# Next operands made later and over more steps, low part last, products in source order

## The chip, the cores and the metric

One core of a Trainium2 chip runs the whole program in one launch. The metric is the device time of one execution in microseconds (us). The kernel before was timed three times: 1541.97 us in the middle, 1541.9 and 1543.53 at the ends.

## The reference, cut to what matters

Attention with pooled keys and values gives tokens x (4608 x 512). Then come two stages of matrix products without biases:

```python
a = x @ w1; b = x @ w2
x2 = (a * b @ w3) @ w_out          # moe_*: d_ff 1024
h = x2 @ w_in                      # moe2_*: 512 x 2048
r = np.maximum(h, 0.0)
out = (r * r) @ w_out2             # moe2_w_out: 2048 x 512
```

All is float32. The change touches the last three lines alone.

## The kernel before

Tokens are cut into nine blocks of 512. A float32 operand is split into a high part, which is the value rounded to the type that TensorE takes (made by ScalarE, a cast), and a low part, the remainder (made by VectorE, a subtraction); `split` (L118 to L120) does both. A product of two operands is three matrix products: high x high, high x low, low x high.

The second stage takes the blocks in pairs (p = 0 to 3; the ninth block is left without a partner and goes last). For a pair, the products with w_in and with w_out are each done by seven products of combinations instead of eight. For w_in, `h_step(p, u, n)` does product n = 0 to 6 of unit u = 0 to 7: six products of 128x128 by 128x512 into one accumulator (ps_a to ps_d), then sums, relu and square, which leave a tile gs. Its moving operands `x2o` are seven combinations B11, T1, T2, T3, B21, B22, T4 of the pair's x2, for two halves each. `operands_of(p)` returns a list: one load, then one `cut` per name. A cut is, for two halves, a difference in place (only for T1 to T4; L1043) and a `split`. So the seven cuts are 8 differences and 14 low parts on VectorE and 14 casts on ScalarE. The tiles x2o have no second set: T1 of the next pair is written over T1 of this one, after its last product.

For w_out, `o_step(p, m, u)` does product m = 0 to 6 of unit u = 0 to 7: three products into each of two accumulators o (L1174). Its moving operand `gt` (high and low part of a gs or of a difference of two gs, which is L1148) is made by `o_prep`, three steps ahead; `cuts` is the list of the low parts made so far. After unit 7 of an m the accumulators are added to sums `so` (L1189, or copied at first by ScalarE, L1205), and for m = 3 to 6 a sum is transposed (L1195) and stored.

Stationary operands come from DRAM through a ring of eight tiles `un`: a step's unit is fetched eight steps ahead, when the step that had the tile has ended. SP issues these loads and all other loads and stores of this part.

`plan()` sets the order of steps: for pair p, the last of the steps with w_in, then one or two steps with w_out that are left over, then twelve steps with w_out of the pair (m = 0 for u = 0 to 7, then m = 1 for u = 0 to 3), then w_in of the next pair in turn with w_out of this one. I call this place a change of pairs. The first (from pair 0 to pair 1) has no w_out left over; in the second and third, one step (m = 6, u = 7) stands ahead of the twelve, so that the ninth of the twelve, (m = 1, u = 0), is the tenth from there.

A scheduler of the framework then orders each engine's instructions: it takes the source's order, but lets an instruction that it thinks ready go ahead of one that it thinks is not. `issue_after(ins, other)` ties one instruction behind another of the same engine, without a wait. The main loop calls the cuts: before, at n = 1, 3, 4, 5, 6 of the last unit and at two later steps with w_out.

Of the kernel before, what the change touches and what calls it, by code (L numbers as in the profile page):

```python
# [15 lines left out]
P = 128  # L16
# [19 lines left out]
def attn_moe_moe2_kernel(  # L36
# [16 lines left out]
    nc = tc.nc  # L53
# [47 lines left out]
    def tick():  # L101
        ticks[0] += 1
        for p in list(pumps):
            p()
# [9 lines left out]
    def f32(ap):  # L114
        return ap.bitcast(F32)

    def split(hi, lo, src, eng=None):

        nc.scalar.copy(hi, src)  # L119
        return (eng or nc.vector).tensor_sub(lo, src, f32(hi))  # L120

    def issue_after(ins, other):

        tc.add_manual_dep(
            ins.ins, other.ins.name, mybir.DependencyInfo(
                mybir.DependencyClass.NoSync, mybir.DependencyReason.DATA),
            reason="queue order")
# [46 lines left out]
    def run_step(steps):  # L174
        for fn in steps.pop(0):
            fn()
# [42 lines left out]
    def fetch():  # L219
        if n_used[0] + len(ahead) < len(useq):  # L220
            key = useq[n_used[0] + len(ahead)]
            while key not in stored:
                run_step(quarters)
            r = ring[0].tile([P, 2, 2, P], F32R, tag="unit", name="un")
            nc.sync.dma_start(f32(r), unit(key))
            ahead.append(r)

    def fetched(key):
        assert useq[n_used[0]] == key, (useq[n_used[0]], key)
        n_used[0] += 1  # L230
        return ahead.pop(0)
# [608 lines left out]
    NU = F2 // P // 2  # L840
# [79 lines left out]
    def out_unit(key):  # L920
        return key.rearrange("p a b c -> p (a b c)").rearrange("p (i c) -> p i c", i=2)
# [41 lines left out]
    def plain_units(u):  # L963
        half, v = divmod(u, NU)
        return [(("A11", "A12"), ("A21", "A22"))[half][x] for x in range(2)], v
# [47 lines left out]
    def drop(name):  # L1013
        slots.append(gs.pop(name))
# [5 lines left out]
    def operands_of(p):  # L1020

        iA, iB = pairs[p]
        raws = {}

        def load():
            for i in range(2):
                for y in range(2):
                    r = raw_x[0] if i and y else raw_p.tile(
                        [P, 2, TB], F32, tag="raw", name="x2r")
                    for x, blk in enumerate((iA, iB)):  # L1030
                        nc.sync.dma_start(r[:, x, :], x2d[blk][:, 2 * y + i, :])
                    raws[i, y] = r

        def cut(name):

            y, x = {"B21": (1, 0), "B22": (1, 1), "T3": (0, 1)}.get(name, (0, 0))
            for i in range(2):
                src = raws[i, y][:, x]
                a, b = {"T1": (raws[i, 0][:, 1], src), "T2": (raws[i, 1][:, 1], src),
                        "T3": (raws[i, 1][:, 1], src), "T4": (raws[i, 1][:, 0], src)}.get(  # L1040
                            name, (None, None))
                if a is not None:
                    nc.vector.tensor_sub(src, a, b)  # L1043
                t = x2o[name, i]
                split(t[:, 0, :], t[:, 1, :], src)

        return [load] + [
            (lambda n=n: cut(n)) for n in ("B11", "T1", "T2", "T3", "B21", "B22", "T4")]

    def plain_operands():  # L1050
        raws = []

        def load():
            for y in range(2):
                r = raw_p.tile([P, 2, TB], F32, tag="raw", name="x2r")
                nc.sync.dma_start(r, x2d[last][:, 2 * y:2 * y + 2, :])
                raws.append(r)

        def cut(kc):
            t = x2o[PLAIN[kc]]  # L1060
            split(t[:, 0, :], t[:, 1, :], raws[kc // 2][:, kc % 2])

        return [load] + [(lambda kc=kc: cut(kc)) for kc in range(KD)]
# [2 lines left out]


    hb = {}

    def run_prods(ps, todo, first):  # L1070
        for j, (l, r) in enumerate(todo):
            nc.tensor.matmul(ps, l, r, start=first and j == 0, stop=j == len(todo) - 1,  # L1072
                             skip_group_check=True)
        fetch()
        tick()

# [58 lines left out]
    ob = {}  # L1135
# [19 lines left out]
    cuts = []  # L1155
# [3 lines left out]
    def sub(t, x):  # L1159


        return t.rearrange("p (j x a) -> p j x a", x=2, a=32)[:, :, x, :]

    def o_step(p, m, u):
        name, x = OPRODS[m]
        if u == 0 and m < 2:
            ob[x] = [ps_acc.tile([P, TB], F32, tag="acc", name=f"o{x}") for _ in range(2)]
        un = out_unit(fetched(("o" + name, u)))
        gt = gts.pop(("o", p, m, u))
        for o in range(2):  # L1170
            os_ = slice(o * P, (o + 1) * P)
            todo = [(un[:, 0, os_], gt[:, 0]), (un[:, 0, os_], gt[:, 1]), (un[:, 1, os_], gt[:, 0])]
            for j, (l, r) in enumerate(todo):
                nc.tensor.matmul(  # L1174
                    ob[x][o], l, r, start=u == 0 and m != 5 and j == 0,
                    stop=u == NU - 1 and j == 2, skip_group_check=True)
        fetch()
        tick()
        g = {2: 2, 4: 1, 5: 4, 6: 3}.get(m)
        if g:  # L1180
            drop((p, u, g))
        if u < NU - 1:
            return
        iA, iB = pairs[p]

        def add(to, src):
            for o in range(2):
                ps = ob[x][o].rearrange("p (j a) -> p j a", a=32)
                nc.vector.tensor_add(sub(sums_o[to], o), ps, sub(sums_o[src], o))  # L1189

        def finish(name, blk, half):

            add(name, name)
            r = sums_o[4]
            nc.vector.transpose(r, sums_o[name])  # L1195
            for i in range(P // 32):
                c0 = i * P + half * 64
                nc.sync.dma_start(
                    out[blk * TB:(blk + 1) * TB, c0:c0 + 64].rearrange("(j a) c -> a j c", a=32),
                    r[i * 32:(i + 1) * 32].rearrange("p (j c) -> p j c", c=64))  # L1200


        if m == 0:
            for o in range(2):
                nc.scalar.copy(sub(sums_o[0], o), ob[x][o].rearrange("p (j a) -> p j a", a=32))  # L1205
        elif m == 1:
            add(1, 0)
        elif m == 2:
            add(2, 0)
            add(3, 1)  # L1210
        elif m == 3:
            add(2, 2)
            finish(3, iB, 1)
        elif m == 4:
            finish(2, iA, 1)
        elif m == 5:
            finish(1, iB, 0)
        else:
            finish(0, iA, 0)
# [99 lines left out]
    for step in order:  # L1319
# [4 lines left out]
        elif step[0] == "ph":  # L1324
            names, x = plain_units(step[2])
# [57 lines left out]
    def prepare():  # L1383
        while n_prep[0] < min(n_out + 3, len(outs)) and ready(outs[n_prep[0]]):
            o_prep(outs[n_prep[0]])
            n_prep[0] += 1

    todo_x = []
    head = False
    for step in order:  # L1390
        if step[0] == "h":
            _, p, u, n = step
            h_step(p, u, n)
            prepare()
            nxt = p + 1
            if u == NU - 2 and n == 0:
                todo_x = operands_of(nxt) if nxt < len(pairs) else plain_operands()
                todo_x.pop(0)()
            if u == 0 and n == 0:
                assert not todo_x  # L1400
                head = False
            if u == NU - 1 and n in (1, 3, 4, 5, 6) and todo_x:
                todo_x.pop(0)()
                head = n == 6
        elif step[0] == "ph":
            ph_step(*step[1:])
            prepare()
        else:
            if step[:3] == ("o", 0, 0) and step[3] == 0:
                while quarters:  # L1410
                    run_step(quarters)
                for _ in range(4):
                    t = prep_p.tile([P, 2, TB], F32, tag="w", name="so")
                    sums_o.insert(0, t.rearrange("p x c -> p (x c)"))
            prepare()
            n_out += 1
            if todo_x and head and step[2:] in ((0, 2), (0, 5), (1, 1), (1, 3)):
                todo_x.pop(0)()
            (o_step if step[0] == "o" else po_step)(*step[1:])
    for p in reversed(late):  # L1420
# [33 lines left out]
```

## Time and profile before

| what | value |
|---|---|
| median of three runs | 1541.97 us |
| the profiled execution | 1548.74 us |
| its span, first to last instruction | 1546.9 us |
| TensorE (PE) busy | 1496.1 us, 97% |
| VectorE (DVE) busy | 986.8 us, 64% |
| ScalarE (ACT) busy | 780.7 us, 50% |
| products and weight loads | 6752 each |

The profile was taken from one execution. A matrix product's record lasts 0.39 us since products overlap; the time that one takes is the distance from start to start. A bracket behind a row of a timeline is idle time ahead of it and what ended it. A count in a window holds every instruction that touches it.

### The profile page before, as it was taken

How to read it: one execution, taken by the hardware profiler on the slowest of the kernel's cores; microseconds unless marked ns; L12 is line 12 of the kernel's file. 1: busy time of each engine (PE TensorE's matmuls, PEld its weight loads, DVE VectorE, ACT ScalarE, POOL GpSimd, SP SyncE). 2: the span in 40 equal slices, each digit the busy share in tenths (PEclk: the TensorE clock that was granted, in tenths of full speed). 3: DMA queues.
4: the chain of work that ended last, by engine and by line, in shares of the span. 5: the costliest groups of instructions: out<-in, count | busy, mean ns of one | idle time of the engine just before them, and what ended most of it. 6: DMA issues, size and time to landing. Idle time of an engine off the chain costs nothing.

```text
span 1546.9 us, 21467 instructions
## 1 busy us (share of the span) xinstructions
PE 1496.1 (97%) x6752; PEld 1199.4 (78%) x6752; DVE 986.8 (64%) x1778; ACT 780.7 (50%) x1905; POOL 82.5 (5%) x146
## 2 busy tenths in 40 slices
PE   5899999989999999999999999999999999999998
PEld 3457777868887888778888777888888888888887
DVE  7897685646666565667245467758775877476642
ACT  6766454434453453646134664456445644464441
POOL 1011011101010010100000000000000000000000
PEclk9999999999999999999999999999999999999999
DMA  9555656646574855777429768778777877798752
GB/s 296 185 156 140 168 175 165 180 121 182 153 223 117 269 159 159 212 227 244 134 90 304 215 185 242 196 218 224 239 203 213 228 209 208 206 269 281 209 161 93
DMA packets 304720, 303.85 MB, mean 196 GB/s; under 512 B 131296, under 2 KB 196832, under 8 KB 304608
## 3 DMA queue, kind: packets, MB, share of 16 engines
q1 hardware_dynamic: 299424, 293.04, 65.3%
q10 hardware_dynamic: 5184, 9.44, 1.7%
q8 instruction: 55, 0.90, 0.3%
q14 instruction: 57, 0.47, 0.1%
HBM read 243.27 MB, written 56.62 MB: 194 GB/s over the span
## 4 chain that ended last, share of the span: by engine, by line
PE 67%; DMA 4%; DVE 4%; ACT 2%; SPq 1%; issue 1%; DVEq 0%; ACTq 0%
PE o L1174 17%; PE ps_w L185 16%; PE acc L185 8%; PE ps_a L1072 5%; PE ps_c L1072 5%; PE ps_d L1072 5%; PE ps_h L185 3%; PE o L185 3%; PE ps_b L1072 2%; DMA raw<-in_moe_w_out_dram 1%; PE ps_s L439 1%; PE ps_av L185 1%; DVE x2o L120 1%; PE ps_t L486 1%; DMA x2d<-st 1%
## 5 line engine op out<-in xcount | busy, mean ns | idle before, releaser
L1174 PE MATMUL o<-gt,un 128*128 128x512 f32 x1344 | 329.7, 390 | 1.4 <-DVE gt L120 1.0
L1174 PEld LDWEIGHTS o<-gt,un 128*128 128x128 f32 x1344 | 251.8, 188 | 55.8 <-DVE gt L120 3.5
L120 DVE TENSOR_TENSOR gt<-gs,gt 128x512 fp32r<-128x512 f32 x240 | 164.7, 688 | 184.0 <-ACT gt L119 182.4
L185 PE MATMUL ps_w<-x,wt 128*128 128x512 f32 x960 | 243.3, 399 | 2.7 <-ACT x L517 1.9
L119 ACT CAST gt<-gs 128x512 fp32r<-128x512 f32 x240 | 148.6, 620 | 156.3 <-PE o L1174 89.8
L185 PE MATMUL acc<-gt,Wt 128*128 128x512 f32 x864 | 219.4, 396 | 3.0 <-ACT st L829 2.8
L185 PEld LDWEIGHTS ps_w<-x,wt 128*128 128x128 f32 x960 | 176.5, 189 | 42.1 <-DVE x L520 3.3
L185 PE MATMUL ps_w<-x,un 128*128 128x512 f32 x768 | 187.9, 393 | 0.0
L185 PEld LDWEIGHTS acc<-gt,Wt 128*128 128x128 f32 x864 | 160.0, 189 | 35.8 <-ACT st L829 4.0
L185 PEld LDWEIGHTS ps_w<-x,un 128*128 128x128 f32 x768 | 142.0, 188 | 29.6 <-issue 1.2
L456 ACT ACTIVATE att<-ps_s,mx 128x72 f32<-128x72 f32 (+1 forms) x320 | 98.0, 324 | 65.0 <-DVE mx L454 64.3
L1079 ACT ACTIVATE r<-r 128x512 f32<-128x512 f32 x96 | 60.6, 632 | 120.0 <-DVE r L1109 119.4
L801 DVE TENSOR_TENSOR gf<-asb,ps_w 128x512 f32<-128x512 f32 x72 | 49.3, 684 | 88.0 <-PE ps_w L185 87.5
L1072 PE MATMUL ps_a<-x2o,un 128*128 128x512 f32 x384 | 98.3, 391 | 3.7 <-ACT p L1097 2.2
L1072 PE MATMUL ps_c<-x2o,un 128*128 128x512 f32 x384 | 98.7, 393 | 0.0
L1072 PE MATMUL ps_d<-x2o,un 128*128 128x512 f32 x384 | 97.7, 390 | 0.0
L119 ACT CAST gt<-gf 128x512 fp32r<-128x512 f32 x72 | 44.8, 623 | 94.0 <-DVE gf L801 92.8
L1080 ACT ACTIVATE gs<-r 128x512 f32<-128x512 f32 x144 | 89.9, 629 | 1.7
L1072 PEld LDWEIGHTS ps_a<-x2o,un 128*128 128x128 f32 x384 | 71.9, 188 | 19.7 <-ACT p L1097 2.6
L1148 DVE TENSOR_TENSOR gs<-gs 128x512 f32<-128x512 f32 x128 | 86.6, 683 | 0.0
L1072 PEld LDWEIGHTS ps_c<-x2o,un 128*128 128x128 f32 x384 | 72.8, 190 | 15.4 <-DVE u L1103 0.3
L1072 PEld LDWEIGHTS ps_d<-x2o,un 128*128 128x128 f32 x384 | 72.4, 189 | 15.1
(109 smaller groups left out, 1943.3 us busy)
## 6 DMA issues: line engine op xcount, KB each, us to landing
un<-u_w SPq DMA_DIRECT2D x128, 256.0 KB
un<-u_A SPq DMA_DIRECT2D x128, 256.0 KB
un<-u_S SPq DMA_DIRECT2D x128, 256.0 KB
un<-u_oS SPq DMA_DIRECT2D x128, 256.0 KB
un<-u_oA SPq DMA_DIRECT2D x96, 256.0 KB
raw<-in_moe_w_dram SPq DMA_DIRECT2D x32, 512.0 KB
raw<-in_moe_w_out_dram SPq DMA_DIRECT2D x24, 512.0 KB
x2d<-st ACTq DMA_DIRECT2D x36, 256.0 KB
```

What stands on the lines that cost most here:

```text
L119: nc.scalar.copy(hi, src)
L120: return (eng or nc.vector).tensor_sub(lo, src, f32(hi))
L185: (lambda a=a, b=b, i=i: nc.tensor.matmul(ps, a, b, start=first and i == 0, stop=last and i == n - 1))
L439: nc.tensor.matmul(ps[:n, x * 2 * SP:(x + 1) * 2 * SP], t[:, hp, c0:c0 + n], kbd[:, hp].rearrange("p a s -> p (a s)"), start=True, stop=True)
L456: nc.scalar.activation(av[:, h0 + h], sv[:, h], ACTF.Exp, bias=mx[:n, h:h + 1], scale=scale, accum_out=sm[:n, h0 + h:h0 + h + 1])
L486: nc.tensor.transpose(ps[:, c, :n], att[g % 2][:n, c * 2 * SP:c * 2 * SP + P], ident[:n, :n])
L801: nc.vector.tensor_mul(gf, asb, pss[1])
L1072: nc.tensor.matmul(ps, l, r, start=first and j == 0, stop=j == len(todo) - 1, skip_group_check=True)
L1079: nc.scalar.activation(t, src, ACTF.Relu)
L1080: nc.scalar.activation(take(name), t, ACTF.Square)
L1148: d = nc.vector.tensor_sub(src, a, src)
L1174: nc.tensor.matmul(ob[x][o], l, r, start=u == 0 and m != 5 and j == 0, stop=u == NU - 1 and j == 2, skip_group_check=True)
```

## The change

Four edits. The main loop makes the next pair's operands at n = 1, 3, 5 of the last unit (B11, T1, T2) and at the steps with w_out m = 0, u = 0, 2, 3, 5 (T3, B21, B22, T4). The first instruction of a cut on VectorE is tied behind the newest low part of a gt. In a step with w_out the products go high x high, low of the weights x high, high x low of gt, each for both accumulators in turn, so that gt's low part is read last. All products of `h_step` and `o_step` are tied into the source's order.

```diff
--- before.py
+++ after.py
@@ -1039,10 +1039,13 @@
                 a, b = {"T1": (raws[i, 0][:, 1], src), "T2": (raws[i, 1][:, 1], src),
                         "T3": (raws[i, 1][:, 1], src), "T4": (raws[i, 1][:, 0], src)}.get(
                             name, (None, None))
+                d = []
                 if a is not None:
-                    nc.vector.tensor_sub(src, a, b)
+                    d.append(nc.vector.tensor_sub(src, a, b))
                 t = x2o[name, i]
-                split(t[:, 0, :], t[:, 1, :], src)
+                d.append(split(t[:, 0, :], t[:, 1, :], src))
+                if cuts:
+                    issue_after(d[0], cuts[-1])
 
         return [load] + [
             (lambda n=n: cut(n)) for n in ("B11", "T1", "T2", "T3", "B21", "B22", "T4")]
@@ -1066,11 +1069,19 @@
 
 
     hb = {}
+    last_mm = []
+
+    def in_turn(ins):
+
+        if last_mm:
+            issue_after(ins, last_mm[0])
+        last_mm[:] = [ins]
 
     def run_prods(ps, todo, first):
         for j, (l, r) in enumerate(todo):
-            nc.tensor.matmul(ps, l, r, start=first and j == 0, stop=j == len(todo) - 1,
-                             skip_group_check=True)
+            in_turn(nc.tensor.matmul(
+                ps, l, r, start=first and j == 0, stop=j == len(todo) - 1,
+                skip_group_check=True))
         fetch()
         tick()
 
@@ -1167,13 +1178,12 @@
             ob[x] = [ps_acc.tile([P, TB], F32, tag="acc", name=f"o{x}") for _ in range(2)]
         un = out_unit(fetched(("o" + name, u)))
         gt = gts.pop(("o", p, m, u))
-        for o in range(2):
-            os_ = slice(o * P, (o + 1) * P)
-            todo = [(un[:, 0, os_], gt[:, 0]), (un[:, 0, os_], gt[:, 1]), (un[:, 1, os_], gt[:, 0])]
-            for j, (l, r) in enumerate(todo):
-                nc.tensor.matmul(
-                    ob[x][o], l, r, start=u == 0 and m != 5 and j == 0,
-                    stop=u == NU - 1 and j == 2, skip_group_check=True)
+        for j, (x1, x2) in enumerate(((0, 0), (1, 0), (0, 1))):
+            for o in range(2):
+                in_turn(nc.tensor.matmul(
+                    ob[x][o], un[:, x1, o * P:(o + 1) * P], gt[:, x2],
+                    start=u == 0 and m != 5 and j == 0,
+                    stop=u == NU - 1 and j == 2, skip_group_check=True))
         fetch()
         tick()
         g = {2: 2, 4: 1, 5: 4, 6: 3}.get(m)
@@ -1399,9 +1409,10 @@
             if u == 0 and n == 0:
                 assert not todo_x
                 head = False
-            if u == NU - 1 and n in (1, 3, 4, 5, 6) and todo_x:
+            if u == NU - 1 and n in (1, 3, 5) and todo_x:
                 todo_x.pop(0)()
-                head = n == 6
+            if u == NU - 1 and n == 6:
+                head = True
         elif step[0] == "ph":
             ph_step(*step[1:])
             prepare()
@@ -1414,7 +1425,7 @@
                     sums_o.insert(0, t.rearrange("p x c -> p (x c)"))
             prepare()
             n_out += 1
-            if todo_x and head and step[2:] in ((0, 2), (0, 5), (1, 1), (1, 3)):
+            if todo_x and head and step[2:] in ((0, 0), (0, 2), (0, 3), (0, 5)):
                 todo_x.pop(0)()
             (o_step if step[0] == "o" else po_step)(*step[1:])
     for p in reversed(late):
```

On TensorE, at the first change of pairs, the order before puts products of the new pair (ps_a) behind the eighth step with w_out (gt_9134 is its operand, gt_9152 that of the ninth):

```order
L1174 MATMUL o_9077<-gt_9134,un 128x512 x3
L1072 MATMUL ps_a<-x2o,un 128x512 x3
L1174 MATMUL o_9181<-gt_9152,un 128x512
L1174 MATMUL o_9182<-gt_9152,un 128x512
L1072 MATMUL ps_a<-x2o,un 128x512 x2
L1174 MATMUL o_9181<-gt_9152,un 128x512 x2
L1174 MATMUL o_9182<-gt_9152,un 128x512 x2
L1174 MATMUL o_9181<-gt_9164,un 128x512 x3
```

After, they stand behind the twelfth step, whose operand is gt_9192 (gt_9178 is the eleventh's):

```order
L1183 MATMUL o_9182<-gt_9178,un 128x512
L1183 MATMUL o_9181<-gt_9192,un 128x512
L1183 MATMUL o_9182<-gt_9192,un 128x512
L1183 MATMUL o_9181<-gt_9192,un 128x512
L1183 MATMUL o_9182<-gt_9192,un 128x512
L1183 MATMUL o_9181<-gt_9192,un 128x512
L1183 MATMUL o_9182<-gt_9192,un 128x512
L1082 MATMUL ps_a<-x2o,un 128x512 x6
L1082 MATMUL ps_b<-x2o,un 128x512 x6
```

Nowhere else does the order of steps on TensorE change; within a step with w_out the two accumulators take turns.

On VectorE, at the second change of pairs, this stands before from the low part of the fourth step with w_out (gt_10471) to that of the ninth (gt_10537); x2o rows are low parts of operands, x2r rows their differences, the gs row is a difference of two gs:

```order
L120 TENSOR_TENSOR gt_10471<-gs,gt_10471 128x512
L120 TENSOR_TENSOR gt_10482<-gs,gt_10482 128x512
L120 TENSOR_TENSOR x2o<-x2r,x2o 128x512
L120 TENSOR_TENSOR gt_10497<-gs,gt_10497 128x512
L120 TENSOR_TENSOR x2o<-x2r,x2o 128x512
L1043 TENSOR_TENSOR x2r<-x2r 128x512
L120 TENSOR_TENSOR gt_10508<-gs,gt_10508 128x512
L1148 TENSOR_TENSOR gs<-gs 128x512
L120 TENSOR_TENSOR x2o<-x2r,x2o 128x512
L120 TENSOR_TENSOR gt_10519<-gs,gt_10519 128x512
L120 TENSOR_TENSOR gt_10537<-gs,gt_10537 128x512
```

After, from the fourth step (gt_10467) to the ninth (gt_10537):

```order
L120 TENSOR_TENSOR gt_10467<-gs,gt_10467 128x512
L120 TENSOR_TENSOR x2o<-x2r,x2o 128x512 x2
L120 TENSOR_TENSOR gt_10478<-gs,gt_10478 128x512
L120 TENSOR_TENSOR x2o<-x2r,x2o 128x512 x2
L120 TENSOR_TENSOR gt_10493<-gs,gt_10493 128x512
L120 TENSOR_TENSOR x2o<-x2r,x2o 128x512 x2
L120 TENSOR_TENSOR gt_10508<-gs,gt_10508 128x512
L120 TENSOR_TENSOR gt_10519<-gs,gt_10519 128x512
L1044 TENSOR_TENSOR x2r<-x2r 128x512 x2
L1159 TENSOR_TENSOR gs<-gs 128x512
L120 TENSOR_TENSOR x2o<-x2r,x2o 128x512 x2
L120 TENSOR_TENSOR gt_10537<-gs,gt_10537 128x512
```

Eleven instructions were between and at these ends, and now seventeen; two more, a pair of x2r, now stand between the transpose (L1205 after, L1195 before) and the first of these rows. Between them and the two sums ahead of the transpose nothing else moved. The third change has the same order.

## Rows read from the trace of the kernel before

**Rows 1.** page: busy time; costliest line (busy, mean ns, idle before)

```profile
PE 1496.1 (97%) x6752; PEld 1199.4 (78%) x6752; DVE 986.8 (64%) x1778; ACT 780.7 (50%) x1905; POOL 82.5 (5%) x146
...
L1174 PE MATMUL o<-gt,un 128*128 128x512 f32 x1344 | 329.7, 390 | 1.4 <-DVE gt L120 1.0
```

**Rows 2.** windows: length, PE, PEld, DVE, ACT, POOL busy, PEclk, DMA share, GB/s

```profile
900.00:1000.00 100.00, 97.57 (x430) 80.17 (x429) 74.50 (x119) 54.01 (x95) 0.00 (x0) 1.00 0.72 209
...
1300.00:1400.00 100.00, 100.00 (x443) 82.82 (x442) 64.45 (x96) 53.89 (x91) 0.00 (x0) 1.00 0.82 238
```

**Rows 3.** chain that ended last, 926 to 941 us: start, us, what

```profile
926.35 4.72 DMA un<-u_A
...
939.58 1.36 PE o L1174 x6
```

**Rows 4.** timeline, TensorE, first change of pairs: start, us, what, count [idle]

```profile
917.35 4.69 PE L1174 MATMUL o<-gt,un 128*128 128x512 f32 x20
923.05 6.64 PE L1174 MATMUL o<-gt,un 128*128 128x512 f32 x28 [1.01 <-DVE gt L120]
931.12 0.97 PE L1072 MATMUL ps_a<-x2o,un 128*128 128x512 f32 x3 [1.42 <-DMA un<-u_A]
931.92 0.62 PE L1174 MATMUL o<-gt,un 128*128 128x512 f32 x2
...
938.05 1.52 PE L1072 MATMUL ps_b<-x2o,un 128*128 128x512 f32 x6
```

**Rows 5.** timeline of TensorE, second and third change of pairs

```profile
1071.33 18.67 PE L1174 MATMUL o<-gt,un 128*128 128x512 f32 x78
1089.84 1.52 PE L1072 MATMUL ps_a<-x2o,un 128*128 128x512 f32 x6
...
1224.48 18.65 PE L1174 MATMUL o<-gt,un 128*128 128x512 f32 x78
1242.97 1.52 PE L1072 MATMUL ps_a<-x2o,un 128*128 128x512 f32 x6
```

**Rows 6.** windows of one step each, TensorE, second change of pairs

```profile
1074.08:1075.44 1.36, 1.36 (x8) 1.00 0.80 200
1075.44:1076.80 1.36, 1.25 (x6) 1.00 0.93 238
```

**Rows 7.** window of VectorE, second change of pairs

```profile
1058.00:1083.00 25.00, 24.97 (x42) 1.00 0.82 228
```

**Rows 8.** timeline of VectorE, second change of pairs

```profile
1074.00 1.28 DVE L1189 TENSOR_TENSOR so<-o,so 128x512 f32<-128x512 f32 x2
...
1075.80 1.23 DVE L1195 STREAM_TRANSPOSE gx<-so 128x1024 f32<-128x1024 f32 x1
1076.96 1.25 DVE L120 TENSOR_TENSOR gt<-gs,gt 128x512 fp32r<-128x512 f32 x2
...
1081.14 0.68 DVE L1148 TENSOR_TENSOR gs<-gs 128x512 f32<-128x512 f32 x1
...
1082.35 1.28 DVE L120 TENSOR_TENSOR gt<-gs,gt 128x512 fp32r<-128x512 f32 x2
```

**Rows 9.** timeline of ScalarE, first, then second change of pairs

```profile
929.05 0.59 ACT L1205 COPY so<-o 128x512 f32<-128x512 f32 x1 [0.58 <-PE o L1174]
929.54 0.62 ACT L119 CAST gt<-gs 128x512 fp32r<-128x512 f32 x1
...
1083.91 0.59 ACT L1205 COPY so<-o 128x512 f32<-128x512 f32 x1 [1.35 <-PE o L1174]
```

**Rows 10.** timeline of TensorE, then windows with granted clock (third figure)

```profile
854.34 1.81 PE L1072 MATMUL ps_a<-x2o,un 128*128 128x512 f32 x6 [2.22 <-ACT p L1097]
...
860.22 1.53 PE L1072 MATMUL ps_a<-x2o,un 128*128 128x512 f32 x6
...
856.00:858.00 2.00, 2.00 (x6) 0.50 0.83 282
...
930.00:932.00 2.00, 0.88 (x4) 1.00 0.93 280
```

## Prediction

> **What bounds the kernel now.** I read the page first: TensorE is busy 97% of the span, VectorE 64%, ScalarE 50% [rows 1]. Only what makes TensorE wait can move the time. Then windows of 100 us over the part that the change touches, from 855 us on: where nothing is missing a window holds 443 products, one per 0.226 us; from 900 to 1000 it holds 430, so 13 x 0.226 = 2.9 us are lost there [rows 2]. A step has six products and takes 1.36 us [rows 3].
>
> The timelines of TensorE say where: at the changes from one pair of token blocks to the next.
> - First change: thirteen steps (twelve with w_out, one with w_in) would take 13 x 1.36 = 17.7 us from 917.35; the next group starts at 938.05, 20.7 us later. Lost: 3.0 us, mostly a wait for a low part and one for a unit of w_in [rows 4].
> - Second and third: 78 products would take 17.7 us, and the next group starts after 18.5 both times. Lost: 0.8 us each [rows 5], with no wait named, but six products in a window of one step where a full one touches eight [rows 6].
> - At the fourth, into the block without a partner, the window from 1300 to 1400 is full [rows 2].
>
> So at most 3.0 + 0.8 + 0.8 = 4.6 us, 0.3% of the span, can be won here. The next view is of what these steps wait for: VectorE. Around the second change it has not a gap in 25 us, 42 instructions at 0.60 us each [rows 7]. At the changes of pairs VectorE is the bound, and TensorE is hidden behind it only as far as VectorE has worked ahead.
>
> **The change part by part.** *Products in the source's order.* The order moves TensorE in one place alone, the first change: before, the first products of the new pair stand after eight steps with w_out, and their unit, fetched only when a step eight places ahead has freed its buffer, is what the 1.42 us wait is for [rows 4]. It was asked for at 926.35 and took 4.7 us [rows 3]. After, they follow twelve steps, 5.4 us later, and the unit is there. The wait goes; what is late next is the low and high part of the ninth step, below.
>
> *The low part last.* The low part is wanted from a step's fifth product instead of its second: 3 x 0.227 = 0.7 us of slack more per step. The products now alternate between two accumulators. Where two in a row did so before, they last 0.62 us [rows 4] where one lasts 0.39 [rows 1]: the second starts 0.23 us behind, as elsewhere, with a weight load for each as before. I cost the alternation at nothing; the rows read to 0.01 us for two, so its ends are 0.005 us on 1344 products [rows 1], 6.7 us to either side, and the row nearest to it (one interval of 0.23 us) is at the middle.
>
> *The operands later.* This is the term that decides. No instruction is added. In the second and third change, before, VectorE has done all but four of the 22 instructions that make the operands (14 low parts, 8 differences) when it comes to the two sums of the last step (L1189). After, the order has twelve of them behind those sums, eight more. Counted in slots of 0.60 us (the transpose, 1.16 us, is two [rows 8]), from the first sum to the low part of the ninth step with w_out: 16 before, 24 after.
> - Before: the sums start at 1074.00 and the low part 15 slots later, 1083.0; the row has it at 1082.95, the second of the two at 1082.35 [rows 8]. So the count is a usable clock.
> - After: the sums wait for the step that starts at 1071.33 and ends 1.36 us later; behind the last sum of the w_in products and two low parts they start at about 1073.3. The low part starts 23 slots later, at 1087.1, and is done at 1087.8.
> - TensorE without any loss would start this step nine steps after 1071.33, at 1083.6, and want the low part 0.9 us later, at 1084.5. It is 3.3 us late. The next step has two differences and a low part, 1.8 us of VectorE against 1.36 us of TensorE: 0.5 us more. VectorE alone makes a loss of 3.8 us.
> - ScalarE adds to it: its cast of the high part waits for the difference g2 - g1 (slot 21, done at 1086.0), and stands behind the copy of the finished sum, which itself waits for TensorE (as at 1083.91 [rows 9]), and behind the cast of the last operand: 0.6 us each. The cast ends near 1087.2, so the step starts 3.7 us late, and the next 0.5 us more: 4.2 us.
> Less the 0.8 us lost before: +3.4 us for each of these two changes. The bounds: VectorE alone, +3.0; every further cast in the way once more (0.6 each at both steps [rows 9]), +4.5; below, if the slack hides all of it, -0.8.
>
> *The first change* has no idle time of VectorE to defer work into: before and after, it works through the same backlog. After, the last sum of w_in products cannot start before 917.5; the low part of the ninth step is the 20th behind it, 917.5 + 12.0 = 929.5, done at 930.2; it is wanted at 917.35 + 8 x 1.36 + 0.9 = 929.1. With the next step that is a loss of 1.5 us from VectorE alone. The high part's cast stands behind the copy that waited for TensorE until 929.05 before [rows 9], and behind one cast more: near 930.2, for a step due at 928.2, then 0.5 us: 2.5 us. I take 2.5 against 3.0, -0.5 us (bounds -1.5, and +0.3 with one more cast of 0.6 us and a little).
>
> *The rest at nothing.* In the fourth change the four operands stand at the same places. On SP's queue the loads of the raw operands move behind some units at each change; units are asked for eight steps ahead, 10.9 us, against 4.7 us to land [rows 3], and the operands of the pair after next are wanted a whole pair later. If that cover went, it would be a wait like the 1.42 us one. POOL has no work here [rows 2].
>
> The sum: -0.5 + 3.4 + 3.4 = +6.3 us. The profiled execution took 1548.7 us (span 1546.9), so it would take 1555.0; the median of the runs shown is 1541.97, 6.8 us less, and I put the same sum on it: 1548.3 us. From the bounds with a loss, 1546.5 to 1551.3.
>
> The spacing of VectorE's instructions is where a rule bears on it. The rows show 0.60 us from start to start, less than the 0.68 us that one lasts [rows 7, 8]. The Trainium skill (VectorE: DVE Perf Modes, "The DRAIN you can't avoid") says that an instruction doesn't start until the one before has left the pipeline, and names as the exception one that nothing holds. By the main rule 24 slots would be 16.3 us, 1.9 us more per change; the trace sides with the exception, and the sum stays at 0.60.
>
> **The rivals.** *The slack hides it (faster).* If the low part's 0.7 us per step and the work done ahead cover VectorE's deferral, all of 4.6 us comes back: 1537.4 us. For it: the waits of the second and third change are for low parts. Against it: it takes 24 slots within the 11.2 us from 1073.3 to 1084.5, so a spacing under 0.47 us, and no row shows one. It decides at the ninth step of the second change: a low part there by 1084.5.
>
> *The clock falls too (slower still).* A wait of 2.22 us for operands was followed by 5.88 us for 18 products in place of 4.08, the clock at 0.50 in between: 1.8 us more. After a wait of 1.42 us it stayed at 1.00 [rows 10]. My sum has three waits of 1.7 to 2.0 us at the ninth step, between the two. If all three lower it: +5.4, 1553.7 us. The Trainium skill (TensorE: Matmul & The Clock Gate, Part 1) says that the slow clock is the default, which activity lifts; the trace agrees in that it fell after a wait, and shows the other outcome as well.
>
> *Nothing to measure.* The first change is cured whole (-3.0) because order was all that it lacked, and the two others lose 1.5 us each since VectorE gets to the sums sooner than I think: 1542 us. For it: the only waits that the profile names are in the first change. Against it: the sums can't start before TensorE's step at 1071.33 is over.
>
> **How the numbers follow.** My forecast has 0.57, the clock 0.20, nothing to measure 0.12, the slack 0.11. A measurement of this kernel tells 0.2%, 3.1 us, from no change; forecast and clock lie beyond it: slower 0.77, same 0.12, faster 0.11. The range of 8 in 10 takes the forecast's bounds, the clock's case, about half of no change, and by that also most of the alternation's upper end: 1541.0 to 1554.0.
>
> **What would show it.** In the changed kernel's profile: at the first change no wait for a unit of w_in; at the second and third, VectorE with gaps before the two sums and none for the 14 us behind them; TensorE waiting up to half a microsecond at the fourth to seventh step with w_out, and nearly 2 us at the ninth, put down to gt by ScalarE or VectorE; the window of 100 us around the second change with some 20 products fewer. I am wrong if the ninth step starts within 1 us of its time, if VectorE's spacing there is not 0.60, or if the steps outside the changes take other than 1.36 us.

## The result and the profile after

The changed kernel took 1557.8 us (median of 4 runs, 1553.83 to 1558.89), the kernel before 1542.68 us beside it (4 runs, 1541.9 to 1543.53). The ratio on record is 1.0086, with a 95% interval of 1.0066 to 1.0107: 13 us more, from 10 to 16 (the two medians lie 15.1 us apart). Forecast were 1548.3 us, with a range of 1541.0 to 1554.0: the direction holds, the size doesn't, and the time lies above the range.

The profiled execution of the changed kernel took 1553.83 us, span 1552.1. First the page's busy times and its costliest line; they answer to [rows 1].

```profile
PE 1496.3 (96%) x6752; PEld 1196.3 (77%) x6752; DVE 985.0 (63%) x1778; ACT 781.9 (50%) x1905; POOL 82.9 (5%) x146
...
L1183 PE MATMUL o<-gt,un 128*128 128x512 f32 x1344 | 333.3, 391 | 10.6 <-ACT gt L119 6.1
```

The same work on every engine, and the mean of a product is 391 ns for 390. Only the idle time before the steps with w_out has grown, from 1.4 to 10.6 us. Windows of 100 us (columns as in [rows 2]) say where:

```profile
900.00:1000.00 100.00, 98.05 (x431) 80.14 (x430) 78.09 (x125) 55.81 (x98) 0.00 (x0) 1.00 0.74 212
1000.00:1100.00 100.00, 95.80 (x414) 76.87 (x413) 67.52 (x105) 54.75 (x96) 0.00 (x0) 1.00 0.73 205
...
1200.00:1300.00 100.00, 95.51 (x413) 76.67 (x412) 74.42 (x118) 55.54 (x97) 0.00 (x0) 1.00 0.71 202
1300.00:1400.00 100.00, 100.00 (x443) 82.77 (x442) 64.54 (x97) 53.27 (x90) 0.00 (x0) 1.00 0.81 230
```

A window without a change of pairs is as full as before (443 products), so the steps themselves cost the same. The windows with the second and third change lack 29 and 30 products. The timeline of TensorE at the first and the second change, which answers to [rows 4, 5]:

```profile
910.08 11.35 PE L1183 MATMUL o<-gt,un 128*128 128x512 f32 x48
922.92 1.66 PE L1183 MATMUL o<-gt,un 128*128 128x512 f32 x6 [1.49 <-ACT gt L119]
...
929.26 1.52 PE L1082 MATMUL ps_a<-x2o,un 128*128 128x512 f32 x6
930.62 1.52 PE L1082 MATMUL ps_b<-x2o,un 128*128 128x512 f32 x6
...
1063.90 5.27 PE L1183 MATMUL o<-gt,un 128*128 128x512 f32 x22
1069.70 1.66 PE L1183 MATMUL o<-gt,un 128*128 128x512 f32 x6 [0.53 <-DVE gt L120]
1072.63 3.46 PE L1183 MATMUL o<-gt,un 128*128 128x512 f32 x12 [1.27 <-DVE gt L120]
1076.25 3.92 PE L1183 MATMUL o<-gt,un 128*128 128x512 f32 x14 [0.15 <-DVE gt L120]
1081.66 1.66 PE L1183 MATMUL o<-gt,un 128*128 128x512 f32 x6 [1.48 <-ACT gt L119]
1083.78 4.37 PE L1183 MATMUL o<-gt,un 128*128 128x512 f32 x18 [0.46 <-ACT gt L119]
1087.99 1.52 PE L1082 MATMUL ps_a<-x2o,un 128*128 128x512 f32 x6
```

A change's loss is the start of the next group, less the start of its first step with w_out, less 13 x 1.36 = 17.68 us: at the second, 1087.99 - 1063.90 - 17.68 = 6.41 us; at the first, where the thirteenth is the step with w_in at 929.26, it is 930.62 - 910.08 - 17.68 = 2.86. The waits named at the second make only 3.89 of the 6.41. A named wait counts from the end of a product's record, which is 0.16 us after the next product is due (0.39 - 0.23), and six products behind a wait last 1.66 us instead of 1.52: a late step loses some 0.3 us more than the wait that is named. The timeline of weight loads shows, besides, late steps for which the merged rows of the products name no wait:

```profile
1072.63 1.22 PEld L1183 LDWEIGHTS o<-gt,un 128*128 128x128 f32 x6 [1.71 <-DVE gt L120]
1074.44 1.22 PEld L1183 LDWEIGHTS o<-gt,un 128*128 128x128 f32 x6 [0.58 <-DVE gt L120]
1076.25 1.22 PEld L1183 LDWEIGHTS o<-gt,un 128*128 128x128 f32 x6 [0.58 <-DVE gt L120]
1078.06 1.68 PEld L1183 LDWEIGHTS o<-gt,un 128*128 128x128 f32 x8 [0.59 <-DVE gt L120]
```

Three times the next six products start 1.81 us later instead of 1.36: three slots of VectorE, one low part of g and two instructions for the operands. There VectorE sets the pace.

| | change 1 | change 2 | change 3 | behind it, to the end |
|---|---|---|---|---|
| before | 3.02 | 0.83 | 0.81 | 303.93 |
| changed | 2.86 | 6.41 | 6.69 | 305.10 |
| more | -0.16 | +5.58 | +5.88 | +1.17 |
| forecast | -0.5 | +3.4 | +3.4 | 0 |

That makes +12.5 us from the first change to the end, within the measured 10 to 16. The stretch ahead of the first change is not used here: it took 910.08 us and, in a second execution of the same kernel, 913.12, and 917.35 in the profiled execution of the kernel before [rows 4].

The +1.17 us are in the last block, where TensorE meets a wait that it did not have before (the window from 1500 to 1510 us touches 41 products where a full one touches 46):

```profile
1498.60 1.52 PE L1183 MATMUL o<-gt,un 128*128 128x512 f32 x6
1500.82 1.65 PE L185 MATMUL o<-x2o,gt 128*128 128x512 f32 x6 [0.71 <-ACT gt L119]
```

What stands behind the second change is read from the chain of waits of the changed kernel (start, us, what), from the last unit of the old pair on:

```profile
1056.46 0.63 ACT x2o L119
1057.12 0.69 DVE x2o L120
1057.81 0.61 DVE r L1120
1058.44 0.64 ACT r L1090
...
1062.30 0.52 ACT gt L119
1062.85 0.69 DVE gt L120
1063.54 0.60 DVE r L1120
...
1068.36 0.68 DVE so L1199
```

From 1053.2 to 1078.0 there is no piece of TensorE in it. VectorE and ScalarE hand the work to each other: the cast of an operand (x2o), its low part, and only behind that the sum r of n = 3, its Relu, a cast of g, the low part of g, the next sum r, and so on to the sums of the output (so). The products that three of these sums r add up are these (n = 3, 5, 6):

```profile
1054.38 1.52 PE L1082 MATMUL ps_d<-x2o,un 128*128 128x512 f32 x6
...
1059.82 1.52 PE L1082 MATMUL ps_c<-x2o,un 128*128 128x512 f32 x6
...
1062.54 1.52 PE L1082 MATMUL ps_d<-x2o,un 128*128 128x512 f32 x6
```

The timeline of VectorE shows what the hand-over costs:

```profile
1057.72 0.68 DVE L1120 TENSOR_TENSOR r<-ps_d,u 128x512 f32<-128x512 f32 x1
1060.28 0.69 DVE L120 TENSOR_TENSOR gt<-gs,gt 128x512 fp32r<-128x512 f32 x1 [1.87 <-ACT gt L119]
1062.85 0.69 DVE L120 TENSOR_TENSOR gt<-gs,gt 128x512 fp32r<-128x512 f32 x1 [1.87 <-ACT gt L119]
1063.45 0.68 DVE L1120 TENSOR_TENSOR r<-ps_c,u 128x512 f32<-128x512 f32 x1
...
1065.96 0.68 DVE L1120 TENSOR_TENSOR r<-ps_d,u 128x512 f32<-128x512 f32 x1
...
1067.76 1.28 DVE L1199 TENSOR_TENSOR so<-o,so 128x512 f32<-128x512 f32 x2
...
1079.72 0.69 DVE L1159 TENSOR_TENSOR gs<-gs 128x512 f32<-128x512 f32 x1
...
1081.73 0.69 DVE L120 TENSOR_TENSOR gt<-gs,gt 128x512 fp32r<-128x512 f32 x1
```

The first sum r starts 1.8 us after its products ended (1054.38 + 1.52 = 1055.90). Then VectorE, which before had no gap in 25 us here [rows 7], is idle for 1.87 us twice. The second time ready work stands behind the low part that waits: the products of the second sum r had ended at 1061.34, and it starts at 1063.45. Before, this sum stood ahead of that low part:

```profile
1070.40 0.68 DVE L1109 TENSOR_TENSOR r<-ps_c,u 128x512 f32<-128x512 f32 x1
1071.00 0.68 DVE L120 TENSOR_TENSOR gt<-gs,gt 128x512 fp32r<-128x512 f32 x1
```

So VectorE comes to the sums 3.86 us after the first step (1067.76 - 1063.90); before it was 2.67 [rows 5, 8].

### The profile page after: what moved, and what is told of

It reads as the page before. It is cut to its first block, busy times and chain, and to the rows that moved or that the text cites. A ratio compares the mean times of both kernels' runs of the same rounds, so it can differ in the third digit from the quotient of the medians.

```text
span 1552.1 us, 21460 instructions
## 1 busy us (share of the span) xinstructions
PE 1496.3 (96%) x6752; PEld 1196.3 (77%) x6752; DVE 985.0 (63%) x1778; ACT 781.9 (50%) x1905; POOL 82.9 (5%) x146
## 4 chain that ended last, share of the span: by engine, by line
PE 74%; DVE 3%; ACT 1%; DMA 1%; issue 1%; SPq 1%; DVEq 0%; ACTq 0%
PE ps_w L185 18%; PE o L1183 18%; PE acc L185 9%; PE ps_a L1082 5%; PE ps_c L1082 5%; PE ps_d L1082 5%; PE ps_b L1082 3%; PE ps_h L185 3%; PE o L185 3%; PE ps_s L439 1%; PE ps_av L185 1%; PE ps_t L486 1%; DVE gt L120 1%; DVE x2o L120 1%; SPq L345 1%
## 5 line engine op out<-in xcount | busy, mean ns | idle before, releaser
L1183 PE MATMUL o<-gt,un 128*128 128x512 f32 x1344 | 333.3, 391 | 10.6 <-ACT gt L119 6.1
```

The costliest lines, as they stand in the source:

```text
L1183: in_turn(nc.tensor.matmul(ob[x][o], un[:, x1, o * P:(o + 1) * P], gt[:, x2], start=u == 0 and m != 5 and j == 0, stop=u == NU - 1 and j = ...
```

## The experiments

Two theories stood at the start. *The sums start late*: in the order that the operands' instructions now have in the last unit, VectorE and ScalarE wait for each other. *The operands behind the sums*: only the number of slots after them counts. All kernels were run in turn with the kernel before. "To the end" is from the first w_out step of the first change to the end of the span, without the stretch that varies.

| kernel | changes 1, 2, 3: lost us | to the end | against before | time (before) | ratio, 95% |
|---|---|---|---|---|---|
| before | 3.02, 0.83, 0.81 | 629.6 | | | |
| changed, again | 2.86, 6.38, 6.68 | 641.9 | +12.3 | 1560.58 (1542.44) | 1.0078 to 1.0132 |
| products only | 2.13, 4.19, 4.19 | 636.5 | +7.0 | 1551.63 (1545.61) | 1.0030 to 1.0064 |
| operands only | -, 6.59, 6.89 | 639.6 | +10.1 | 1555.77 (1545.61) | 1.0057 to 1.0090 |
| no tie | 2.26, 4.19, 4.19 | 636.6 | +7.1 | 1552.53 (1545.61) | 1.0036 to 1.0081 |
| old places | 2.13, 4.93, 4.89 | 638.0 | +8.4 | 1550.93 (1545.61) | 1.0027 to 1.0060 |
| low part last only | 1.72, 4.20, 4.19 | 636.1 | +6.6 | 1550.63 (1542.44) | 1.0030 to 1.0063 |
| in turn only | 2.66, 0.85, 0.89 | 629.3 | -0.2 | 1543.27 (1542.44) | 0.9992 to 1.0020 |
| sum first | 2.37, 4.95, 5.26 | 638.6 | +9.0 | 1551.53 (1542.44) | 1.0038 to 1.0081 |
| low last, old queues | 2.15, 0.20, 0.20 | 628.6 | -1.0 | 1542.92 (1542.68) | 0.9986 to 1.0014 |

Every "against before" lies within the interval of its ratio (0.1% is 1.5 us). The first change of operands only can't be read in this way, since steps are mixed there.

**Changed, again.** The same kernel.

> 

> The changed kernel once more, beside the parts of it, so that they are compared on one chip. All theories: the loss at the second and third change of pair is again 6.3 to 6.8 us each and at the first 2 to 3 us, since the orders on the engines are the same; the time is 7 to 12 us over the kernel before. If it were 3 us or less over it, the first measurement would have been of the front part, whose length differs between executions, and not of the change.

The losses repeat to 0.03 us. Its median is 18 us over the kernel before (interval of the ratio: 12 to 20) where 7 to 12 were expected, and more than its trace has (12.3, at the lower end): whether its timed executions lose something else is open.

**Products only.** The operands at their old places and not tied.

```diff
-                if cuts:
-                    issue_after(d[0], cuts[-1])
-            if u == NU - 1 and n in (1, 3, 5) and todo_x:
+            if u == NU - 1 and n in (1, 3, 4, 5, 6) and todo_x:
-            if todo_x and head and step[2:] in ((0, 0), (0, 2), (0, 3), (0, 5)):
+            if todo_x and head and step[2:] in ((0, 2), (0, 5), (1, 1), (1, 3)):
```

> 

> The changed kernel with the operands made at the steps of before and without the tie behind the newest low part; kept are the low part last and the products in the source's order. Theory (VectorE's deferred operands make the loss): VectorE's order then has one of the 22 operand instructions behind the sums at the second and third change of pairs, against 4 in the kernel before and 12 in the changed one, so these two changes lose under 0.8 us each; at the first change the wait for the unit of w_in is gone and 2 to 3 us remain. 1539.5 to 1542.5 us. Rival (products alternating between two accumulators, or tied into the source's order, cost the time): as slow as the changed kernel, 1553 to 1559 us, with steps of more than 1.36 us.

Theory and rival both missed. With all operands' work but one low part ahead of the sums, the second and third change still lose 4.19 us each, before any operand can be late. The timeline of TensorE at the second change:

```profile
1065.76 1.52 PE L1181 MATMUL o<-gt,un 128*128 128x512 f32 x6
1068.21 1.67 PE L1181 MATMUL o<-gt,un 128*128 128x512 f32 x6 [0.93 <-ACT gt L119]
1070.71 1.66 PE L1181 MATMUL o<-gt,un 128*128 128x512 f32 x6 [0.83 <-ACT gt L119]
1073.32 14.47 PE L1181 MATMUL o<-gt,un 128*128 128x512 f32 x60 [0.95 <-ACT gt L119]
```

The second to fourth step here, which are the first three of the twelve, each wait for a high part, and then none does. ScalarE's timeline shows why they are late:

```profile
1059.40 2.26 ACT L119 CAST x2o<-x2r 128x512 fp32r<-128x512 f32 x4 [2.34 <-DVE x2r L1044]
1063.80 0.63 ACT L1088 ACTIVATE r<-r 128x512 f32<-128x512 f32 x1 [2.13 <-DVE r L1118]
...
1065.00 0.60 ACT L119 CAST gt<-gs 128x512 fp32r<-128x512 f32 x1
```

It stood idle for 4.5 us, because VectorE did nine of the operands' instructions in a row before the sum r. From here on the theory was: the order of VectorE's and ScalarE's queues in the last unit costs, and two parts of the change spoil it, each on its own.

**Operands only.** The products as before; the operands later and tied.

```diff
-        if last_mm:
-            issue_after(ins, last_mm[0])
...
-        for j, (x1, x2) in enumerate(((0, 0), (1, 0), (0, 1))):
-            for o in range(2):
+        for o in range(2):
+            for j, (x1, x2) in enumerate(((0, 0), (0, 1), (1, 0))):
```

> 

> The kernel before with the operands as in the changed kernel (later steps and the tie) and the products as before, low part second, order left to the scheduler. Theory: the second and third change lose what they lose in the changed kernel (6.4 and 6.7 us) and, without the 0.7 us of slack in a step, up to 1 us more each: 1556 to 1561 us. Rival (the products cost the time): 1541 to 1544 us.

Just under the range; the losses at the second and third change are those of the whole change.

**No tie.** The changed kernel, with the operands at their new places in the source, not tied.

```diff
-                if cuts:
-                    issue_after(d[0], cuts[-1])
```

> 

> The changed kernel without the tie of a cut's first instruction behind the newest low part; the later steps stay. Without the tie VectorE's order at the second and third change is that of e1: the scheduler takes the operands forward past the sums. Theory, sharpened (the tie holds the operands back, the steps at which they are called do not): 1539.5 to 1542.5 us. Rival (the later steps alone hold them back): 1550 to 1558 us.

**Old places.** The changed kernel, with the operands tied, at their old places.

```diff
-            if u == NU - 1 and n in (1, 3, 5) and todo_x:
+            if u == NU - 1 and n in (1, 3, 4, 5, 6) and todo_x:
-            if todo_x and head and step[2:] in ((0, 0), (0, 2), (0, 3), (0, 5)):
+            if todo_x and head and step[2:] in ((0, 2), (0, 5), (1, 1), (1, 3)):
```

> 

> The changed kernel with the operands called at the steps of before, the tie kept. VectorE's order has 6 of the 22 behind the sums at the second and third change, and five instructions between the last sum of w_in products and them. Theory: the low part of the ninth step with w_out is 18 slots of 0.60 us behind the first sum (24 in the changed kernel), which starts some 1.7 us later than in the kernel before relative to TensorE: a loss of 2 to 3 us at each, 1543.5 to 1548 us. Rival (the tie costs nothing, the steps do): 1540 to 1543 us.

Without the tie the new places change nothing against products only: the scheduler moves the work forward again, and the time missed what was expected. With the tie at the old places a change loses 0.7 us more than without, with the new places a further 1.5 to 1.8. Of old places a loss of 2 to 3 us was expected and it was 4.9; the time lies above what was expected, too. VectorE's timeline shows why:

```profile
1073.17 1.28 DVE L1199 TENSOR_TENSOR so<-o,so 128x512 f32<-128x512 f32 x2
```

TensorE's first step is at 1067.01, so the sums start 6.16 us after it where 2.67 + 1.7 = 4.4 were expected. The low part of the ninth step follows them by 10.15 us, 17 slots, as expected. So the start of the sums was sized too small here as well, by 1.8 us. And since the change loses less than in the changed kernel, though the sums start later, start and slots behind it have to be added up; neither decides alone.

**Low part last only.** The kernel before, with this alone:

```diff
-        for o in range(2):
-            os_ = slice(o * P, (o + 1) * P)
-            todo = [(un[:, 0, os_], gt[:, 0]), (un[:, 0, os_], gt[:, 1]), (un[:, 1, os_], gt[:, 0])]
...
+        for j, (x1, x2) in enumerate(((0, 0), (1, 0), (0, 1))):
+            for o in range(2):
```

> 

> Of the change only that the steps with w_out take g's low part last; operands' places, their tie and the scheduler's freedom over the products are as before. Theory (the low part last makes the scheduler put VectorE's operands ahead of the sum of n=3, and ScalarE starves behind it): loss at the second and third change 4.2 us each, as with the tie removed, the time 5 to 8 us over the kernel before. Rival (the loss of 4.2 us came from the products kept in the source's order): losses near 0.8 us at both, the time within 1.5 us of the kernel before.

**In turn only.** The kernel before, with every product tied behind the one before it in the source:

```diff
+        if last_mm:
+            issue_after(ins, last_mm[0])
```

> 

> Of the change only that the products keep the source's order; operands, their tie and the order of the three products of a w_out step are as before. Theory (VectorE's and ScalarE's order is then that of the kernel before, and only the products at the first change move): losses 1.6 to 2.5 us at the first change (3.0 before) and 0.8 us at the other two, the time 0 to 1.5 us under the kernel before. Rival (the source's order of the products costs at the changes): losses of 4 us or more at the second and third, the time 5 us or more over the kernel before.

The theory held in both at the second and third change; the time of low part last only is 8.2 us over the kernel before where 5 to 8 were expected, and in turn only lies 0.8 over where 0 to 1.5 under were expected (interval: 1.2 under to 3.1 over). It is the low part last, not the source's order of the products, that costs there, and it does so with no operand moved in the source: the scheduler now puts the operands' work ahead of the sum r, as in products only. That it does so because the low part is now wanted later is my reading of it. "In turn only" gains 0.4 us at the first change, too little to time, and its loss of 2.66 us there lies just above the 1.6 to 2.5 expected.

**Low last, old queues.** Products only, with VectorE's and ScalarE's instructions around the changes tied into the order that they have in "in turn only" (on ScalarE nearly so).

```diff
+        for row in _ORDER:
+            for x, y in zip(row, row[1:]):
+                tc.add_manual_dep(
+                    by[f"I-{y}"], f"I-{x}", _mybir.DependencyInfo(
+                        _mybir.DependencyClass.NoSync, _mybir.DependencyReason.DATA),
+                    reason="queue order")
```

_ORDER holds the instructions' numbers, in the order wanted, for each stretch that differs.

> 

> The products-only kernel (g's low part last, products in the source's order, operands where they were and not tied) with one thing added: on VectorE and ScalarE the instructions around the changes are tied into the order that they have where g's low part is not last, instruction for instruction on VectorE, nearly so on ScalarE. TensorE's order is that of the products-only kernel. Theory (the 4.2 us lost at the second and third change there came from the order in which VectorE and ScalarE then stand, not from the order of the products itself): losses of 0 to 0.9 us at the second and third change, 1.3 to 2.3 us at the first, and from the first w_out step of the first change to the end 627 to 629.5 us (629.6 in the kernel before, 636.5 in the products-only kernel); the time from 2.5 us under to 1 us over the kernel before. Rival (taking the low part last costs by itself): losses of 3 us or more at the second and third change, 635 us or more to the end, 5 us or more over the kernel before.

The same products in the same order on TensorE as in products only, and the loss falls from 4.19 to 0.20 us. The chain of waits at the second change is TensorE alone:

```profile
1065.88 17.89 PE o L1181 x78
1083.77 1.36 PE ps_a L1080 x6
```

So the order of the queues is shown to be the cause of the 4.2 us. The slack of the low part is real too: 0.85 us (in turn only) against 0.20. It is worth 0.65 us at the second and third change each. With 0.9 us less than before at the first, and about 1.1 us given back in the last block, where the wait of 0.71 us is there again, that makes -1.0 us in all against the kernel before, too little to time. No kernel here beats the kernel before measurably.

**Sum first.** The changed kernel, with the first operand behind the sum r.

```diff
+            hb["r"] = nc.vector.tensor_add(t, ps, hb["u4" if n == 3 else "u2"])
...
+                if name == "T1" and "r" in hb:
+                    issue_after(d[-1], hb["r"])
```

> 

> The changed kernel, except that T1's difference and low parts are tied behind the sum r of n=3 in the last unit on VectorE, so that ScalarE's Relu and Square of n=3 don't wait for T1's two low parts. Theory (the sums of the output start late because VectorE and ScalarE wait for each other in the last unit): the sums start 1 to 2 us earlier against the first w_out step than in the changed kernel (3.9 us after it there), and the losses at the second and third change fall from 6.4 and 6.7 us to 4.3 to 5.5 us; the time 2 to 4 us under the changed kernel. Rival (only the number of slots behind the sums decides, and their start does not depend on the order in the last unit): the losses stay at 6.3 to 6.8 us.

VectorE's timeline at the second change:

```profile
1060.85 0.68 DVE L1122 TENSOR_TENSOR r<-ps_d,u 128x512 f32<-128x512 f32 x1
1061.45 1.28 DVE L120 TENSOR_TENSOR x2o<-x2r,x2o 128x512 fp32r<-128x512 f32 x2
1063.40 0.69 DVE L120 TENSOR_TENSOR gt<-gs,gt 128x512 fp32r<-128x512 f32 x1 [0.67 <-ACT gt L119]
...
1070.87 1.28 DVE L1201 TENSOR_TENSOR so<-o,so 128x512 f32<-128x512 f32 x2
```

The first of the two idle times shrinks from 1.87 to 0.67 us. TensorE's first step is at 1068.46, so the sums start 2.41 us after it instead of 3.86: 1.45 us earlier, and the loss falls by 1.46 us (6.41 to 4.95). With the same slots behind the sums, the late start passes to TensorE one for one. The time fell by more than the 2 to 4 us expected (9 us between medians, 3.3 to the end), which goes with what is open on the changed kernel's median.

## Why the prediction was wrong

- **The step that failed** is the start of the sums in "The operands later": "behind the last sum of the w_in products and two low parts they start at about 1073.3", 1.97 us after the first step's start (1073.3 - 1071.33). This has the last sum r start as soon as TensorE's products are there, and costs at nothing, without naming a cover, what the move does in the last unit. The sums started after 3.86 us: the products of the last sum r end 0.16 us after the first step's start (1062.54 + 1.52 - 1063.90), but r starts 2.06 us after it (1065.96), at the end of the hand-over between VectorE and ScalarE, where a wait in one queue became a wait in the other. So all that follows came 1.9 us later, and the ninth step started 1081.66 - 1063.90 - 9 x 1.36 = 5.5 us late where I had 3.7. Sum first shows that taking back part of the late start takes back as much of the loss. I had named gaps of VectorE before the two sums as a sign, and given them no cost; none of my three signs of being wrong came, and none of them asked when the sums start.
- **The clock of slots held.** From the sums to the difference's end I had 12.7 us (1086.0 - 1073.3); it was 12.65. From the sums to the low part of the ninth step I had 23 slots, 13.8 us; it was 13.97, with 0.60 us from start to start and one wait of some 0.2 us for the last operand's cast. The trace sides again with the exception that the Trainium skill names (VectorE: DVE Perf Modes, "The DRAIN you can't avoid"); by its main rule 23 slots of 0.68 us would be 15.6 us, an estimate. ScalarE's cast of the ninth step stood behind the copy and the last operand's cast as said. The step behind it added 0.76 us where I had 0.5.
- **The size**: each of the two terms of +3.4 us measured +5.6 and +5.9, above the upper bound of 4.5. My bounds held only what lies behind the sums.
- **The low part last** was read as slack only. The slack is there (0.65 us per change), but the same edit lets the scheduler reorder VectorE, and that alone costs 4.2 - 0.85 = 3.4 us per change. This is nearly the size of my term, by chance: low part last only loses as much as I forecast, with no operand moved. In the changed kernel it does not add up with the rest: operands only, without the low part last, loses 6.59 and 6.89 us, as much as the whole change.
- **First change**: -0.16 for -0.5, within its bounds. The wait for a unit of w_in is gone, and the ninth step is late instead, as said.
- **The rest at nothing**: right for the alternation (443 products in a window, steps of 1.36 us); wrong for the last block, +1.2 us. Low part last brings it: the kernels with it have the wait of 0.71 us there, and in turn only and operands only are without it (303.97 and 304.00 us behind the third change). No wait of TensorE from 905 us on is put down to a DMA, so the loads on SP's queue cost nothing that shows.
- **Rivals.** The clock did not fall: waits of 1.48 and 1.49 us were followed by a granted clock of 1.00, as the window at the ninth step of the second change shows (third figure; it is 1.00 in all windows of 2 us from 904 to 1536 us):

```profile
1082.00:1084.00 2.00, 1.54 (x7) 1.00 0.18 67
```

The slack did not hide it, and the case of no change needed the sums to come sooner than I took; they came later.

## What to carry to other kernels

When work moves to another place on an engine with an in-order queue, cost the place where it arrives as well as the place that it leaves: ask of each moved instruction what ready work stands behind it, and which engine that work feeds. A count of slots gives a duration; where it starts needs a count of its own. A later due time is not only slack: where a scheduler orders by readiness or need, compare the full order of every engine before and after, at the place and ahead of it. Where executions differ elsewhere, measure a local change by local distances of the trace (here one change of pairs, good to some 0.03 us), not by the whole time.

## What the hardware showed that was not expected

- Two executions of one program reach the same point 3.0 us apart: the first change of the changed kernel starts at 910.08 and 913.12 us. From there on they agree to 0.2 us over 642. The granted clock does not tell them apart: up to 904 us, 2 us x (1 - granted clock), added up over windows of 2 us, is 6.8 us in both, in part at other places. The cause stays open. In the profiled execution of the kernel before, which is there at 917.35 us, the same sum is 10.3 us: a part of that later start goes with the clock.
- The waits that the trace names on TensorE's products can fall far short of a loss (3.89 of 6.41 us): a late step loses some 0.3 us more than its wait, and where every step waits a little, the idle time stands at the weight loads, 0.58 us a step.
